# Attention and two MoE layers in one kernel: zero products on TensorE at the start, later weight conversion, and the first MoE units among the last pair's work

## The chip, the cores and the metric

One core of a Trainium2 chip runs the whole kernel in one launch. The metric is the device time in microseconds. Names of engines: PE is TensorE, DVE is VectorE, ACT is ScalarE, POOL is GpSimd, SP is the engine whose queue issues most DMAs.

## The reference

```python
def _attn_ref(q, k, v):                 # q, k, v: (4, 8, 576, 64) float32
    # rotary embedding on q and k: [x1*cos - x2*sin, x1*sin + x2*cos]
    scores = scale * np.matmul(q_rot, k_rot.transpose(0, 1, 3, 2))
    scores = scores - np.max(scores, axis=-1, keepdims=True)
    attn = np.exp(scores)
    attn = attn / (np.sum(attn, axis=-1, keepdims=True) + 1e-09)
    return np.matmul(attn, v)

x = attn_out.transpose(0, 2, 1, 3).reshape(2304, 512)
h = np.maximum(x @ w_in, 0.0)           # w_in (512, 2048), w_out (2048, 512)
x = (h * h) @ w_out
h = x @ w_in2                           # the second layer, alpha (2048,)
g = np.maximum(h, 0.0) + alpha * np.minimum(h, 0.0)
out = g @ w_out2
```

The weights arrive as 64-bit floats and are turned into 32-bit pairs on the chip.

## The kernel before

**Attention** goes over 16 pairs (one batch, two heads; a head in each half of the 128 partitions). For a pair POOL applies the rotary embedding (`rope`), PE transposes q and k (`turn`, steps KQ, X), ACT writes their rounded high part and DVE the residue (KH, KL, XK, XL, XQ, QL). `scores` (S) makes a block of 128 queries for one head, three matmuls for each half of the keys; the fifth block (i = 4) holds both heads' last 64 queries and reads the tile `qt` beside `nat`. DVE takes its maximum (`top`, R), ACT the exponential with its row sums (`exps`, E). PE transposes the exponentials (`trans`, T; U and W for tails) into banks of PSUM, ACT or DVE copy them out (C, CU, CW), and PE multiplies them with v (`pv`, PV). `store` (ST) and `over_leave` (OR) send the product and the inverse sums to DRAM.

The order on PE, POOL, DVE and ACT is written out by hand. `PLAN` gives each step of a pair a time in a period of 14.053 parts and for some an engine; pair n's step stands at n + time / 14.053 on a common axis, `at` pushes it into a heap, and `run` issues all in order of time. A pair's steps reach over nearly three periods, so up to four pairs overlap. The steps before time 0 of pair 0 are issued by hand at the start: k's rope, its transposes, then q in two parts (columns r = 0, 1 first), with the first score block between them. PSUM has eight banks: four for scores, three for transposes (`bank`), one (`acc`) for the products.

**The MoE layers** go by units. A unit of the first layer is one chunk of 128 hidden columns for 384 tokens: 12 matmuls (`products`, L785 to L787), a rectifier and a square on ACT (`finish`). The first 32 units take two token blocks by turns, so that unit t needs chunk t // 2. `Weights` converts a chunk in stages: load, `convert` and `mask` on DVE, `grow` on ACT, `sign` on DVE, `join` on ACT and DVE; six DVE instructions and two on ACT. Each unit has a list of such stages to issue behind it. The tokens of the first two blocks are read back from DRAM, multiplied by the inverse sums, rounded and split on POOL (`load_x`, `join_x`, `high_x`, `low_x`), through two buffers.

`moe` is a generator: attention resumes it by the event `follow`, 17 times for the tokens' split from 13.8 on (every 0.12 periods), then 11 times. The conversion of chunks 0 to 3 is spread over steps -9 to -1 of it. Two units (`EARLY`) are issued by the last two resumptions, at 17.9, behind everything of attention; the rest follows when attention is done. The scores' banks become the units' four banks (`ps_h`) after the last score; the other four (`ps_y`) are for the second product.

Of the kernel before, what the change touches and what calls it, by code (L numbers as in the profile page):

```python
# [56 lines left out]
AHEAD_X = 17  # L57
X_AT, X_EVERY = 13.8, .12
FOLLOW_AT = 15.5, 15.65, 15.9, 16.05, 16.2, 16.35, 16.5, 16.65, 16.8, 17.9, 17.91
ET = mybir.EngineType  # L60
FIRST_DONE = "KQ", "KH", "KL", "X0", "X1", "XK", "XL", "XQ", "QL", "S0", "R0", "E0"
MANUAL = {ET.PE, ET.Pool, ET.DVE, ET.Activation}


def attention(tc, q, k, v, ident_d, rope_d, xd, rd, follow):
# [10 lines left out]
    with ExitStack() as at:  # L76
        pool = lambda name, bufs, **kw: at.enter_context(tc.tile_pool(name=name, bufs=bufs, **kw))
        front = at.enter_context(ExitStack())
        fpool = lambda name, bufs, **kw: front.enter_context(tc.tile_pool(name=name, bufs=bufs, side="right", **kw))
        pp = pool("aP", NP_)  # L80
        pt = pool("apt", PTB)
        sm = pool("asm", 2)
        st_ = pool("asums", 1)
        ident = st_.tile([P, P], F32, name="ident")
        lds = [fpool("ald0", 1)]
# [24 lines left out]


        raw = {(x, nm): (st_ if nm == "v" else lds[0]).tile([P, 4, 5, D], F32, name=f"{nm}raw{x}") for x in range(2) for nm in "kqv"}
        for x in range(2):
# [18 lines left out]

        def first_rope(nm, r0, r1):

            w, E = r1 - r0, V
            x = raw[0, nm][:, 0:2, r0:r1]
            c, ns, s = (tab[:, r0:r1, i].unsqueeze(1).to_broadcast([P, 2, w, HALF]) for i in range(3))
            if (0, nm) not in rot:
                rot[0, nm] = rp.tile([P, 5, 2, D], F32, name=f"rot{nm}")
            r = rot[0, nm][:, r0:r1].rearrange("p r j d -> p j r d")  # L140
            t1, t2 = (rt.tile([P, 2, 5, D], F32, name=f"f{i}", bufs=1)[:, :, 0:w] for i in (1, 2))
# [181 lines left out]
        def over_leave(n):  # L323
            b, hp = pairs[n]
            r = sm.tile([9, P], F32, name="ri")
            A.activation(out=r, in_=turned.pop((n, "o"))[0:9, 0:P], func=AF.Copy)
            for j in range(2):
                nc.sync.dma_start(out=rd[hp, j, b * S:b * S + 512].rearrange("(i p) -> i p", i=4), in_=r[4 * j:4 * j + 4, :])
            nc.sync.dma_start(out=rd[hp:hp + 1, :, b * S + 512:b * S + 576], in_=r[8:9, :].rearrange("o (j c) -> o j c", j=2))

# [10 lines left out]
        def store(n, hf, side):  # L341
            b, hp = pairs[n]
            ready = n in sts
            if not ready:
                sts[n] = sm.tile([P, S], F32, name="st", bufs=1)
            high(sts[n][:, hf * SH:(hf + 1) * SH], acc.pop((n, hf))[:, 0:SH], side)
            if ready:
                nc.sync.dma_start(out=xd[:, hp, b * S:(b + 1) * S], in_=sts.pop(n))

# [10 lines left out]
        def run():  # L360
            while events:
                t, _, f, a = heapq.heappop(events)
                f(*a)

        def whole(gen):
# [23 lines left out]
        load(0, "q", 2, 4)  # L389
        first_rope("k", 0, 5)  # L390
        first_rope("q", 0, 2)
        for h in range(2):
            whole(turn(0, h, "k"))
            turn_high(0, h, "A", "k")
        whole(turn_tail(0, 0))
        ktail_high(0, "A")
        for h in range(2):
            turn_low(0, h, "k")
        ktail_low(0)
        for c0, c1 in ((0, 2), (2, 4)):  # L400
            if c0:
                first_rope("q", 2, 5)
                for kind, j in itertools.product("RE", range(2)):
                    queue(0, f"{kind}0{j}")
                run()
            for h in range(2):
                whole(turn(0, h, "q", c0, c1))
                turn_high(0, h, "A", "q", c0, c1)
            for h in range(2):
                turn_low(0, h, "q", c0, c1)  # L410
            if c0 == 0:
                for j in range(2):
                    queue(0, f"S0{j}")
                run()
                tables()
        whole(turn_tail(0, 1))
# [8 lines left out]
        for n in range(2, pairs_n):  # L425
            for w, name in ("k", "X0"), ("q", "X1"):
                at(n - 2 + PLAN[name][0] / PERIOD + .25 * (w == "k") + .01, rope, n, w)
            if n % 2 == 0 and n > 2:
                at(n - 3 + PLAN["X1"][0] / PERIOD + .02, load, n // 2, "k")
                at(n - 3 + PLAN["X1"][0] / PERIOD + .02, load, n // 2, "q")  # L430
                at(n - 3 + max(PLAN[x][0] for x in ("PV04", "PV14")) / PERIOD + .01, load, n // 2, "v")

        for n in range(pairs_n):
            for name in PLAN:
                if n or name[:2] not in FIRST_DONE:
                    queue(n, name)
        at(pairs_n - 3 + PLAN["X1"][0] / PERIOD + .02, front.close)
        at(pairs_n - 1 + max(PLAN[x][0] for x in PLAN if x[0] in "REKXQ" or x in ("S40", "S30", "S31")) / PERIOD + .001, scored.close)
        for x in range(AHEAD_X):
            at(X_AT + X_EVERY * x, follow)  # L440
        for x in FOLLOW_AT:
            at(x, follow)
        run()


NB, W = 6, 384
FIRST = 2
STEPS_AHEAD, EARLY = 8, 2
# [71 lines left out]
def moe(tc, xd, rd, mats, pbias, dram, al, out):  # L520
# [11 lines left out]
    with ExitStack() as mo:  # L532
# [240 lines left out]
        def products(u):  # L773
# [84 lines left out]
        conv = [[(d, lambda *j, f=f: f(st, *j)) for d, f in stages] for stages in weights.stages]  # L858
        before = {}
        for k in range(2 * FC):  # L860
            if k < HELD0:
                for d, (_, stage) in zip(FIRST_AT[k], conv[0][1:]):
                    if d < -STEPS_AHEAD - 1:
                        before.setdefault(AHEAD_X + STEPS_AHEAD + 1 + d, []).append((stage, (0, 0, k)))
                    else:
                        jobs.setdefault(d, []).append((0, stage, (0, 0, k)))
                continue
            at = EARLY + EVERY0 * (k - HELD0)
            if k >= FC + OUT0 + OUTX:
# [26 lines left out]
        for e in range(AHEAD_X):  # L896
# [4 lines left out]
            if e in (4, 6):  # L901
                weights.load(st, 0, 0, e // 6)
            for stage, j in before.get(e, []):
                stage(*j)
            yield
# [8 lines left out]
        for t in range(-STEPS_AHEAD - 1, NU + 1):  # L914
# [14 lines left out]
            unfinished += [t - 1] if 0 <= t - 1 < NU and not (t < NU and units[t][0] and units[t][2:] == (0, 0)) else []  # L929
            if "g0" in late:  # L930
                while unfinished:
                    finish(unfinished.pop(0))
# [3 lines left out]
            if t == at_unit[0, NB - 1, 1, 0]:  # L936
                open_two()
            for d, stage, j in sorted(jobs.get(t, []), key=lambda x: x[0]):
                stage(*j)
            if 0 <= t < NU:  # L940
# [8 lines left out]
def fused_kernel(ctx: ExitStack, tc: tile.TileContext, q, k, v, w_in1, w_out1, w_in2, w_out2, alpha, ident_d, rope_d, out):  # L949
# [9 lines left out]
    rest = moe(tc, xd, rd, ((w_in1, w_out1), (w_in2, w_out2)), pbias, dram, al, out)  # L959
    early = iter(range(AHEAD_X + STEPS_AHEAD + 1 + EARLY))  # L960

    def follow():
        if next(early, None) is not None:
            next(rest)

# [37 lines left out]
```

## Time and profile before

| | us |
|---|---|
| median of 3 runs (1070.88 to 1072.12) | 1071.8 |
| the profiled execution | 1077.4 |
| its span, first to last instruction | 1075.6 |
| PE busy in the span | 1035.5 (96%) |
| DVE busy | 717.6 (67%) |
| ACT busy | 584.6 (54%) |
| POOL busy | 379.8 (35%) |
| first unit of the MoE layers starts | 288.35 |

The profiled execution is 5.6 us longer than the median of the others. Times in the rows count from the first instruction. A PE record may be part of a product in 32-bit floats: one `pv` call on one half of the array leaves two records. PE and its weight load (PEld) overlap, and consecutive matmuls overlap by their ends.

### The profile page before, as it was taken

The page shows a single profiled execution, that of the slowest core. Times are in us where ns is not written, and L with a number is a line of the kernel's source. Part 1 is how long each engine was busy: PE and PEld are TensorE (multiplying, and loading weights), DVE is VectorE, ACT ScalarE, POOL GpSimd, SP SyncE. Part 2 cuts the span into 40 slices and gives each one's busy share as a digit, 9 for nine tenths or more (in the row PEclk, how much of TensorE's full clock was granted, in tenths as well). Part 3 has the DMA queues.
Part 4 walks back from the last instruction along what each step waited for, and adds up shares of the span by engine and source line. Part 5 has one row for each costly group of instructions (what it writes and reads, how often), then busy time and mean ns, then how long its engine had stood idle before and what let it go on. Part 6 is the DMA issues. An engine that isn't in the chain of part 4 may idle for free.

```text
span 1075.6 us, 19735 instructions
## 1 busy us (share of the span) xinstructions
PE 1035.5 (96%) x7296; PEld 927.4 (86%) x7296; DVE 717.6 (67%) x1270; ACT 584.6 (54%) x1283; POOL 379.8 (35%) x363
## 2 busy tenths in 40 slices
PE   4899999998999999999999999999999999999997
PEld 3677777775699999999999999899889998899886
DVE  5688888888489977797988876545444463644521
ACT  3688888886378644644646554444343442434321
POOL 6866667636000001332404223355311560136200
PEclk9899999998799999999999999899999999999999
DMA  7022232135434424556565566898214860268111
GB/s 187 2 79 68 90 90 77 60 104 168 127 117 139 134 89 135 186 184 215 192 213 198 185 205 217 316 301 268 63 59 139 254 216 1 59 210 253 37 30 30
DMA packets 101136, 153.21 MB, mean 142 GB/s; under 512 B 16944, under 2 KB 61360, under 8 KB 101040
## 3 DMA queue, kind: packets, MB, share of 16 engines
q1 hardware_dynamic: 100480, 151.41, 44.8%
q8 instruction: 58, 0.95, 0.4%
q10 hardware_dynamic: 560, 0.54, 0.2%
q14 instruction: 38, 0.31, 0.1%
HBM read 114.61 MB, written 37.30 MB: 141 GB/s over the span
## 4 chain that ended last, share of the span: by engine, by line
PE 62%; DVE 5%; DMA 3%; issue 2%; POOL 1%; ACT 1%; SPq 1%; POOLq 0%; DVEq 0%; ACTq 0%
PE py L804 23%; PE ph L697 16%; PE ph L804 8%; PE ph L787 5%; PE ph L785 5%; PE ph L786 5%; DVE gl L738 1%; DMA w<-in_moe_w_in_dram 1%; DVE m L494 1%; DMA xt<-x 1%; DVE m L493 1%; DMA w<-x 1%; DVE w L508 0%; DVE w L596 0%; DMA w<-in_moe_w_out_dram 0%
## 5 line engine op out<-in xcount | busy, mean ns | idle before, releaser
L738 DVE TENSOR_TENSOR gl<-g,gh 128x384 fp32r<-128x384 f32 x189 | 127.6, 680 | 118.0 <-PE py L804 97.0
L697 PE MATMUL ph<-T,xs 128*128 128x384 f32 x1008 | 175.9, 335 | 0.0
L697 PEld LDWEIGHTS ph<-T,xs 128*128 128x128 f32 x1008 | 175.1, 188 | 0.5 <-ACT w L689 0.2
L731 ACT ACTIVATE gh<-g 128x384 fp32r<-128x384 f32 x189 | 97.9, 521 | 142.0 <-PE py L804 137.8
L804 PE MATMUL py<-gh,w 128*128 128x384 f32 x560 | 145.7, 334 | 0.0
L260 DVE TENSOR_REDUCE nm<-sc 128x1 f32<-128x576 f32 x144 | 107.4, 755 | 38.7 <-PE sc L255 36.6
L785 PE MATMUL ph<-xs,held 128*128 128x384 f32 x384 | 128.3, 334 | 0.0
L786 PE MATMUL ph<-xs,held 128*128 128x384 f32 x384 | 128.3, 334 | 0.0
L787 PE MATMUL ph<-xs,held 128*128 128x384 f32 x384 | 128.3, 334 | 0.0
L255 PE MATMUL sc<-nat 64*128 64x288 f32 x768 | 120.0, 322 | 4.8 <-ACT p L269 4.3
L269 ACT ACTIVATE p<-sc,nm 128x576 f32<-128x576 f32 x144 | 105.6, 735 | 25.1 <-DVE nm L260 25.0
L255 PEld LDWEIGHTS sc<-nat 64*128 64x128 f32 x768 | 105.1, 201 | 7.1 <-ACT p L269 6.4
L804 PE MATMUL py<-w,gh 128*128 128x512 f32 x336 | 103.6, 389 | 0.0
L804 PEld LDWEIGHTS py<-gh,w 128*128 128x128 f32 x560 | 101.5, 188 | 0.0
L755 POOL TENSOR_TENSOR xt<-xt 128x384 f32<-128x384 f32 x24 | 27.9, 1166 | 197.0 <-DMA xt<-x 160.1
L804 PE MATMUL py<-gl,w 128*128 128x384 f32 x280 | 94.1, 336 | 3.2 <-DVE gl L738 3.1
L277 PE MATMUL ps<-ident,p 64*128 64x64 f32 x1152 | 92.8, 236 | 1.1 <-DVE ptt L177 1.1
L685 POOL TENSOR_TENSOR g<-g,m 128x384 f32<-128x384 f32 x62 | 67.8, 1101 | 74.0 <-ACT g L684 73.9
L277 PEld LDWEIGHTS ps<-ident,p 64*128 64x128 f32 x1152 | 83.6, 148 | 8.8 <-issue 7.4
L338 PE MATMUL acc<-pt,vraw 128*64 128x288 f32 x512 | 83.8, 441 | 0.9 <-ACT pt L175 0.6
L503 ACT ACTIVATE w<-w,pbias 128x512 uint32<-128x512 uint32 x64 | 48.7, 761 | 48.0 <-DVE w L499 43.7
L804 PEld LDWEIGHTS py<-w,gh 128*128 128x128 f32 x336 | 63.0, 188 | 13.1
(148 smaller groups left out, 2118.4 us busy)
## 6 DMA issues: line engine op xcount, KB each, us to landing
xs<-ws SPq DMA_DIRECT2D x168, 256.0 KB
w<-in_moe_w_in_dram SPq DMA_DIRECT2D x32, 512.0 KB
w<-in_moe_w_out_dram SPq DMA_DIRECT2D x32, 512.0 KB
ws<-w SPq DMA_DIRECT2D x40, 256.0 KB
wk<-xs SPq DMA_DIRECT2D x16, 512.0 KB
w<-wk SPq DMA_DIRECT2D x14, 512.0 KB
x<-st SPq DMA_DIRECT2D x16, 288.0 KB
xt<-x SPq DMA_DIRECT2D x24, 192.0 KB
```

Of the source, the lines that this page charges most:

```text
L255: T.matmul(t[:, x, 0:SH], lhsT=lhs, rhs=k[b][h, c0:c0 + SH], start=y == 0, stop=y == 2)
L260: V.tensor_reduce(out=nm[n, i, j], in_=sc[n, i, j][:, :, 0:SH], axis=AX.XY, op=ALU.max, negate=True)
L269: A.activation(out=Pt[n, i][:, j * S:(j + 1) * S].rearrange("p (a b) -> p a b", a=2), in_=sc.pop((n, i, j))[:, :, 0:SH], func=AF.Exp, bias ...
L277: T.transpose(u[:, 64 * k:64 * k + 64], Pt[n, i][halves[h], c0:c0 + P], ident[halves[h], halves[h]])
L338: T.matmul(acc[n, hf][64 * j:64 * j + 64, 0:SH], lhsT=v2[:, j, c], rhs=t, start=c == 0, stop=c == 4)
L697: T.matmul(bank[c], lhsT=w[:, y0, ws_], rhs=t[:, y1], start=first_ and kc == 0 and n == 0, stop=kc == 1 and n == 2, skip_group_check=not f ...
L731: A.activation(out=hi, in_=hidden(layer, b, i), func=AF.Copy)
L738: V.tensor_tensor(out=lo, in0=hidden(layer, b, i), in1=gsp[u][0].bitcast(F32), op=ALU.subtract)
L785: T.matmul(ph[:, :W], lhsT=wh[:, cs], rhs=xh, start=(c == 0), stop=False)
L786: T.matmul(ph[:, :W], lhsT=wh[:, cs], rhs=xl, start=False, stop=False)
L787: T.matmul(ph[:, :W], lhsT=wl[:, cs], rhs=xh, start=False, stop=(c == KC - 1))
L804: T.matmul(acc, lhsT=x, rhs=y, start=(s0 and k == 0), stop=(s1 and k == 2))
```

## The change

- The q rope is done in one piece behind the k rope, and POOL copies one element of its result (`last`) ahead of its own ropes. The tables are built ahead of both.
- PE runs products and transposes of a tile of zeros: 7 products (`spin`, two matmuls each) at the start and 2 behind k's transposes (`WARM`); then, for three pairs that don't exist (-3 to -1), a product in the place of each PV and eight transposes in the place of each T, from time 0 to the place of pair 0's first PV.
- The tokens' split starts at 13.5 instead of 13.8. The 25 further resumptions have written places in the last pair's period, in its plan's parts. Chunk 0 is converted from 12.91 on (the last maximum stands at 12.465), one stage per resumption.
- Four units are issued within attention, at 17.51, 20.9, 26.44 and 39.87. The four after them write the banks of `ps_y`.
- The stores of the last two pairs are issued by ACT's queue instead of SP's. The pool of exponentials (`aP`) is placed behind two others.

```diff
-X_AT, X_EVERY = 13.8, .12
-FOLLOW_AT = 15.5, 15.65, 15.9, 16.05, 16.2, 16.35, 16.5, 16.65, 16.8, 17.9, 17.91
+X_AT, X_EVERY = 13.5, .12
+FOLLOW_AT = (0, 12.38, 12.91, 14.33, 14.34, 15.59, 15.63, 17.51, 17.52, 17.68, 17.69, 19.61, 20.89, 20.9, 21.23, 24.16, 24.17, 25.21, 26.43, 26.44, 28.94, 29.68, 29.69, 31.73, 33.66, 39.87)
-FIRST_DONE = "KQ", "KH", "KL", "X0", "X1", "XK", "XL", "XQ", "QL", "S0", "R0", "E0"
+FIRST_DONE = "KQ", "KH", "KL", "X0", "X1", "XK", "XL", "XQ", "QL"
+WARM = 7, 2
...
+        zeros, last = st_.tile([P, SH], F32, name="zeros"), st_.tile([P, 1], F32, name="last")
+        idle = ps_a.tile([P, 512], F32, name="acc")
+        G.memset(zeros, 0.0)
...
+            eng = nc.scalar if n + 2 >= pairs_n else nc.sync      # over_leave; likewise in store
...
+        def spin():
+            for j in range(2):
+                T.matmul(idle[64 * j:64 * j + 64, 0:SH], lhsT=zeros[:, 0:64], rhs=zeros, start=True, stop=True)
+
+        def idle_turns(h):
+            u = bank()
+            for k in range(8):
+                T.transpose(u[:, 64 * k:64 * k + 64], zeros[halves[h], 0:P], ident[halves[h], halves[h]])
+                yield
...
-        first_rope("k", 0, 5)
-        first_rope("q", 0, 2)
+        tables()
+        for _ in range(WARM[0]):
+            spin()
+        first_rope("k")
         for h in range(2):
             whole(turn(0, h, "k"))
             turn_high(0, h, "A", "k")
         whole(turn_tail(0, 0))
         ktail_high(0, "A")
+        for _ in range(WARM[1]):
+            spin()
+        first_rope("q")
+        G.tensor_copy(out=last, in_=rot[0, "q"][:, 4, 1, 0:1])
         for h in range(2):
             turn_low(0, h, "k")
         ktail_low(0)
-        for c0, c1 in ((0, 2), (2, 4)):
...
+        for h in range(2):
+            whole(turn(0, h, "q"))
+            turn_high(0, h, "A", "q")
+        for h in range(2):
+            turn_low(0, h, "q")
...
+        for n in range(-3, 0):
+            for name in PLAN:
+                t = n + PLAN[name][0] / PERIOD
+                if t < 0 or t > min(PLAN[x][0] for x in PLAN if x[:2] == "PV") / PERIOD:
+                    continue
+                if name[:2] == "PV":
+                    at(t, spin)
+                elif name[0] == "T":
+                    steps(t, .063, idle_turns(int(name[2])), 8)
...
-        for x in FOLLOW_AT:
-            at(x, follow)
+        for x in FOLLOW_AT[1:]:
+            at(pairs_n - 1 + x / PERIOD, follow)
...
-STEPS_AHEAD, EARLY = 8, 2
+STEPS_AHEAD, EARLY = 0, 4
-FIRST_AT = (-9, -9, -9, -8, -8), (-7, -7, -7, -6, -6), (-5, -5, -5, -4, -4), (-3, -3, -3, -2, -2)
+FIRST_AT = -1, 0, 1, 2
...
-                ph = ps_h.tile([P, 512], F32, name="ph")
+                borrowed = EARLY <= u < EARLY + 4
+                ph = late["ps_y"].tile([P, 512], F32, name=f"py{u - EARLY}") if borrowed else ps_h.tile([P, 512], F32, name="ph")
...
-            at = EARLY + EVERY0 * (k - HELD0)
+            at = EARLY - 2 + EVERY0 * (k - HELD0)
...
+            for stage, j in first_jobs.get(t, []):
+                yield
+                stage(*j)
```

## Rows read from the trace of the kernel before

**Rows 1.** Waits of PE from 288 us on: total us, times, longest.
```profile
PE py L804 <- DVE gl L738: 4.5, 4, 1.8
```

**Rows 2.** Timeline, PE: start us, us, tiles; fifth score blocks of pairs 0, 1, 2, 14, 15.
```profile
29.51 1.81 PE L255 MATMUL sc<-nat,qt 128*128 128x288 f32 x6 [1.41 <-ACT p L269]
...
46.13 1.81 PE L255 MATMUL sc<-nat,qt 128*128 128x288 f32 x6 [1.41 <-ACT p L269]
...
63.19 1.05 PE L255 MATMUL sc<-nat,qt 128*128 128x288 f32 x6
...
240.97 1.05 PE L255 MATMUL sc<-nat,qt 128*128 128x288 f32 x6
...
259.20 1.32 PE L255 MATMUL sc<-nat,qt 128*128 128x288 f32 x6 [4.14 <-ACT p L269]
```

**Rows 3.** Windows, PE alone: stretch, its length, busy (instructions), granted clock, DMA.
```profile
44.00:46.00 2.00, 0.71 (x16) 0.69 0.04 8
...
50.00:52.00 2.00, 2.00 (x34) 0.60 0.00 0
```

**Rows 4.** Timeline, the start of pair 0.
```profile
5.86 1.70 DVE L144 TENSOR_TENSOR f<-kraw,tab 128x320 f32<-128x320 f32 x4 [5.86 <-DMA kraw<-in_k_dram]
...
7.59 0.82 DVE L145 TENSOR_TENSOR rotk<-f,f 128x640 f32<-128x640 f32 x1
...
9.72 0.94 DVE L183 TENSOR_TENSOR nat<-ps,nat 128x256 fp32r<-128x256 f32 x3
...
11.36 2.46 PE L255 MATMUL sc<-nat 64*128 64x288 f32 x12 [0.37 <-ACT nat L175]
11.55 3.17 DVE L144 TENSOR_TENSOR f<-qraw,tab 128x192 f32<-128x192 f32 x4
...
11.88 1.70 POOL L157 TENSOR_TENSOR t<-kraw,tab 128x640 f32<-128x640 f32 x1 [7.98 <-DMA kraw<-in_k_dram]
```

**Rows 5.** Timeline, PE: products with v at half and at full clock.
```profile
275.14 4.11 PE L338 MATMUL acc<-pt,vraw 128*64 128x288 f32 x16
...
285.77 2.16 PE L338 MATMUL acc<-pt,vraw 128*64 128x288 f32 x16 [0.56 <-ACT pt L175]
```

**Rows 6.** Timeline, POOL and DVE, tokens' split and first conversion.
```profile
233.93 1.01 POOL L755 TENSOR_TENSOR xt<-xt 128x384 f32<-128x384 f32 x1 [11.06 <-DMA xt<-r]
...
252.98 1.13 DVE L493 TENSOR_SCALAR m<-w 128x512 uint32<-128x512 uint32 x1
```

**Rows 7.** Windows: length, busy of PE, PEld, DVE, ACT, POOL, granted clock, DMA.
```profile
256.00:258.00 2.00, 0.00 (x0) 0.00 (x0) 1.85 (x4) 1.00 (x2) 1.94 (x2) 1.00 0.37 124
...
264.00:266.00 2.00, 2.00 (x24) 2.00 (x24) 0.79 (x2) 1.65 (x3) 0.00 (x0) 0.50 0.71 198
...
280.00:282.00 2.00, 1.71 (x16) 0.90 (x14) 0.22 (x1) 0.56 (x2) 0.00 (x0) 0.93 0.21 70
```

**Rows 8.** Groups by line, PE, from 259 to 288.35: busy us, mean ns, idle.
```profile
L338 PE MATMUL acc<-pt,vraw 128*64 128x288 f32 x64 | 13.5, 560 | 0.9 <-ACT pt L175 0.6 <-ACT st L175 0.3
L277 PE MATMUL ps<-ident,p 64*128 64x64 f32 x88 | 9.1, 300 | 1.1 <-DVE ptt L177 1.1
```

**Rows 9.** Timeline, a change of kind and eight transposes at full clock.
```profile
281.40 0.14 PEld L307 LDWEIGHTS ps<-ident,p 64*128 64x128 f32 x1 [0.44 <-issue]
...
281.52 0.66 PE L277 MATMUL ps<-ident,p 64*128 64x64 f32 x8
```

**Rows 10.** The chain that ended last, one of the units' matmuls: start us, us.
```profile
299.91 0.17 PE ph L787
```

**Rows 11.** Timeline, DVE: first and last of a chunk's six instructions.
```profile
274.31 0.42 DVE L493 TENSOR_SCALAR m<-w 128x512 uint32<-128x512 uint32 x1
...
277.93 0.69 DVE L515 SCALAR_TENSOR_TENSOR held<-m,w 128x512 fp32r<-128x512 f32 x1
```

**Rows 12.** Timeline, issues of two small stores; the first rectifier.
```profile
281.65 0.76 SPq L328 DMA_DIRECT2D r<-ri  x2
...
291.74 0.49 ACT L828 ACTIVATE g<-ph 128x384 f32<-128x384 f32 x1 [2.67 <-DMA r<-ri]
```

More of the change, by code (lines that the diff above doesn't have):

```diff
@@ L79, in attention @@
         fpool = lambda name, bufs, **kw: front.enter_context(tc.tile_pool(name=name, bufs=bufs, side="right", **kw))
-        pp = pool("aP", NP_)
         pt = pool("apt", PTB)
@@ L83, in attention @@
         st_ = pool("asums", 1)
+        pp = pool("aP", NP_)
         ident = st_.tile([P, P], F32, name="ident")
@@ L131, in load, with first_rope @@
             eng.dma_start(out=t[halves[nm == "q"], :, 4], in_=src[:, 512:576, :].rearrange("h p d -> p h d"))
[L133 to L141, printed above, removed]
+        def first_rope(nm):
+            E, w = V, 5
+            x = raw[0, nm][:, 0:2]
+            c, ns, s = (tab[:, 0:5, i].unsqueeze(1).to_broadcast([P, 2, w, HALF]) for i in range(3))
+            rot[0, nm] = rp.tile([P, 5, 2, D], F32, name=f"rot{nm}")
+            r = rot[0, nm].rearrange("p r j d -> p j r d")
+            t1, t2 = (rt.tile([P, 2, 5, D], F32, name=f"f{i}", bufs=1) for i in (1, 2))
             lo, hi = slice(0, HALF), slice(HALF, D)
@@ L326, in over_leave @@
             A.activation(out=r, in_=turned.pop((n, "o"))[0:9, 0:P], func=AF.Copy)
+            eng = nc.scalar if n + 2 >= pairs_n else nc.sync
             for j in range(2):
-                nc.sync.dma_start(out=rd[hp, j, b * S:b * S + 512].rearrange("(i p) -> i p", i=4), in_=r[4 * j:4 * j + 4, :])
-            nc.sync.dma_start(out=rd[hp:hp + 1, :, b * S + 512:b * S + 576], in_=r[8:9, :].rearrange("o (j c) -> o j c", j=2))
+                eng.dma_start(out=rd[hp, j, b * S:b * S + 512].rearrange("(i p) -> i p", i=4), in_=r[4 * j:4 * j + 4, :])
+            eng.dma_start(out=rd[hp:hp + 1, :, b * S + 512:b * S + 576], in_=r[8:9, :].rearrange("o (j c) -> o j c", j=2))
         def pv(n, hf, c):
@@ L347, in store @@
             if ready:
-                nc.sync.dma_start(out=xd[:, hp, b * S:(b + 1) * S], in_=sts.pop(n))
+                (nc.scalar if n + 2 >= pairs_n else nc.sync).dma_start(out=xd[:, hp, b * S:(b + 1) * S], in_=sts.pop(n))
         pairs_n = len(pairs)
@@ L399, in attention @@
         ktail_low(0)
-        for c0, c1 in ((0, 2), (2, 4)):
[L401 to L415, printed above, removed]
+        for h in range(2):
[3 more added lines that the diff above has]
+            turn_low(0, h, "q")
         whole(turn_tail(0, 1))
@@ L858, in moe @@
         conv = [[(d, lambda *j, f=f: f(st, *j)) for d, f in stages] for stages in weights.stages]
-        before = {}
+        first_jobs = {}
         for k in range(2 * FC):
             if k < HELD0:
[L862 to L866, printed above, removed]
+                first_jobs.setdefault(FIRST_AT[k], []).extend((stage, (0, 0, k)) for _, stage in conv[0][1:])
                 continue
-            at = EARLY + EVERY0 * (k - HELD0)
+            at = EARLY - 2 + EVERY0 * (k - HELD0)
             if k >= FC + OUT0 + OUTX:
@@ L902, in moe @@
                 weights.load(st, 0, 0, e // 6)
-            for stage, j in before.get(e, []):
-                stage(*j)
             yield
@@ L929, in moe @@
             unfinished += [t - 1] if 0 <= t - 1 < NU and not (t < NU and units[t][0] and units[t][2:] == (0, 0)) else []
+            if t == EARLY:
+                for d, stage, j in sorted(jobs.pop(t, []), key=lambda x: x[0]):
+                    stage(*j)
             if "g0" in late:
@@ L938, in moe @@
             for d, stage, j in sorted(jobs.get(t, []), key=lambda x: x[0]):
+                stage(*j)
+            for stage, j in first_jobs.get(t, []):
+                yield
                 stage(*j)
@@ L959, in fused_kernel @@
     rest = moe(tc, xd, rd, ((w_in1, w_out1), (w_in2, w_out2)), pbias, dram, al, out)
-    early = iter(range(AHEAD_X + STEPS_AHEAD + 1 + EARLY))
     def follow():
-        if next(early, None) is not None:
-            next(rest)
+        next(rest)
     attention(tc, q, k, v, ident_d, rope_d, xd, rd, follow)
```

## The prediction

> **What bounds the kernel now.** I read the waits first. From 288 us to the end TensorE (PE) waits for DVE 4.5 us in four places and otherwise runs through [rows 1]: the two MoE layers are a train of matmuls, and what moves their start moves the end by as much. So only the time before 288 us is open, and there I read the timeline for one row that recurs once per pair, the fifth score block (out sc, in nat,qt) [rows 2]. From pair 2 to pair 14 it comes every (240.97 - 63.19) / 12 = 14.82 us. Three stretches miss that pace. Pair 0 needs until 29.51; pairs 1 and 2 come after 16.62 and 17.06 us; pair 15 after 18.23.
>
> Next the clock. [...] Before pair 15's fifth block PE waits 4.14 us for one exponential [rows 2], whose maximum stands on DVE behind the conversion of the first weight chunk (1.13 us for an instruction that takes 0.42 when GpSimd is quiet) [rows 6, 11]. PE is empty for a whole window; after it the clock is 0.50 for some 20 us, although PE is busy for 2.00 of 2.00 us, and it rises at about 280.3 [rows 7].
>
> **The change, part by part.** Sums are against the profiled execution: span 1075.6, its own time 1077.4; the median of the other runs is 1071.8, and I subtract the saving from that.
>
> *The start.* The k rope stays: four multiplies in 1.70 us and an add of 0.82, from 5.86 to 8.41 [rows 4], gated by DMA. The q rope is now whole and takes the same 2.52 us, to about 10.95. In the kernel before its second part took 3.17 us for four multiplies of 192 columns, against 1.70 for four of 320, because GpSimd's own rope ran beside it [rows 4]; the one-element copy called last now holds GpSimd's rope until q is done, which is before 11.88, where it started anyway [rows 4], so pair 1's rope is not later. The tables move to an idle ScalarE before 9 us: free, since DVE's rope is what the next step waits for. Behind the q rope DVE has three k residues (0.94 us in all), the first of which frees the bank for q's transposes at 11.3; transposes, copies and residues of k took from 8.41 to 10.66, 2.25 us, and the first score needs only the transposes and copies of q, some 1.3. First scores therefore at about 12.6 instead of 11.36 [rows 4]: 1.2 lost. What is gained is that nothing is left behind them: block 1 no longer waits for a second half of q.
>
> The zeros' memset lies in the 5.86 us in which DVE waits for DMA [rows 4]: free. Seven zero products are 28 records; at half clock a record is 4.11 / 16 = 0.257 us, at full clock 2.16 / 16 = 0.135 [rows 5], 3.8 to 7.2 us in all; begun by 1.5 they end by 8.7 at the latest, and the first real transpose is ready at 8.4. Cost between 0 and 0.3 us; I take 0. Two more (0.5 to 1.0 us) lie while DVE ropes q: free.
>
> *Until the third pair.* 19 zero products and 80 zero transposes stand in the places that the missing earlier pairs' would have. PE then carries what it carries in the steady state, and the pace of that is 14.82 us a pair, which is less than 16.62 and 17.06, because those were at half clock with PE waiting for ScalarE. From the first score to the fifth block the plan has 12.24 of 14.05 parts of a period, 12.9 us. So the fifth blocks come at 25.5, 40.3 and 55.1 instead of 29.51, 46.13 and 63.19: 8.1 us earlier from pair 2 on. Bounds: 9 if unpaired slots (there are no zeros for sums and tails) let PE run ahead; the other end is below nothing, if PE stays at half clock with more to do (rival 3). I take 8.1, the steady state's own pace.
>
> *The last pair's scores.* The activations' split begins 0.3 periods earlier. GpSimd stood idle 11.06 us before its first multiply for it [rows 6], so it starts earlier by about that and is done about when the fifth block of pair 15 comes; the first conversion is put behind the last maximum. The 4.14 us wait goes and pair 15 takes 14.82 instead of 18.23: 3.4 saved. At most 4.1 [rows 2]; at the least 0 if the eight splits, each of which waits for the one two before on SP's queue, still beat with DVE.
>
> *The tail.* Before: 29.15 us from pair 15's fifth block (259.20) to the first unit (288.35), then four units. A unit is 12 matmuls of 0.17 us [rows 10], 2.1 us with what 0.17 leaves off; four are 8.3. So 37.5 us until the fifth unit. After: the four stand among the tail's products. PE's own work at full clock is 80 records of products at 0.135 = 10.8, about 100 transposes at 0.66 / 8 = 0.08 = 8.0 (88 in the main row) [rows 5, 8, 9], the fifth block 1.1: 19.9 if nothing overlaps, some 17 as the ends of groups overlap; with units 25 to 28. Changing between kinds costs 0.44 us of idle at full clock [rows 9], about ten times: 4.4, partly the cover of the copies. I take 30.5, saving 7.0. The low end of the saving is 0, the tail at half clock as now; the high end 12, PE without a gap. DVE would hold it at about 21 us: four conversions of six instructions, 0.42 to 0.69 us each, 3.4 per chunk without GpSimd beside it [rows 11], 13.4; half of a fifth chunk 1.5; two maxima and the copies some 6. So DVE is no bound, but units 0 and 2 stand in PE's queue ahead of real products and wait for chunks 0 and 1: the chain of one chunk was 4.3 us (274.31 to 278.62) [rows 11], and unit 0 stands 4.6 plan parts (4.9 us) behind its first instruction: a margin of 0.6 us.
>
> Stores of the last two pairs go from SP to ScalarE's queue: past the weight load that now waits on SP for a buffer. An issue is 0.38 us for a small one [rows 12], four per pair, 1.7 us of a ScalarE that is half idle there. At the end they stand ahead of the first rectifiers, and four units' worth of those (0.49 us each and a square) come at once, some 5.5 us with the issues. The next four units go to other banks and cover 8.3 us. Before, the first rectifier itself waited 2.67 us for such a store [rows 12]. The ninth unit needs chunk 4, whose join on ScalarE stands behind the burst: I charge 0.5.
>
> [...]
>
> Sum: 8.1 + 3.4 + 7.0 - 0.5 = 18.0 us. 1077.4 becomes 1059.4, the median 1053.8.
>
> **Rivals.** (1) *The clock falls between warm-up and scores.* From 8.4 to 12.6 PE has two groups of transposes and the two zero products, about half of the time, little more than in the window of the fall at 44.8 [rows 3]. Then the first 5.5 us of scores run at half speed, as from 46.13 to 51.6, 2.7 us lost: 1056.5. For it speaks that fall; against it, the stretch is shorter. (2) *Conversions gate the units.* PE stands at unit 0 or 2, the clock falls as it did behind the empty window, and the tail saves 1 to 3 instead of 7: 1059. For it: DVE was busy 1.85 of 2 us in that window [rows 7]; against: GpSimd no longer slows it. (3) *Slower: zeros that are paid at half clock.* If they fail to raise the clock, PE has two pairs' scores, 108 matmuls at 0.24 = 26 us (between 2.46 / 12 = 0.205 [rows 4] and 1.81 / 6 = 0.30 [rows 2], which has their end in it), and 19 x 4 x 0.257 = 19.5 us of zeros before pair 1's fifth block: 58 instead of 46.13, 12 later, and with ten changes of kind at double price 16. The rest gives 9.9 back: 6 us slower, 1078. It decides from about 20 us on, by whether the score matmuls there still take 0.24 us. Against it: at 51.6 the clock did rise under a mix of scores, transposes and products; for it: transposes and products alone kept PE busy from 264 to 280 at 0.50 [rows 7].
>
> [...]
>
> (4) *GpSimd is late.* Pair 1's two ropes take about 10 us from 11.0 (1.70 for the first of four instructions [rows 4], the two halves about one more, the add one more); their transposes come at about 22.5. If that rope or its bank is late by 3 us, every pair behind is: 1057. (5) *It doesn't do what it says*: the steady pace was set by something that zeros don't change and only the end gains: 1062.
>
> **How the numbers follow.** Forecast 0.50 (own range 1050.5 to 1056); rival 1 0.16; rival 2 0.13; rival 3 0.07; rival 4 0.06; rival 5 0.04; anything else 0.04, on either side. About 0.2%, 2.1 us, is what a measurement here can tell from no change. Faster: all but rival 3 and half of the rest, less a few for sums of two rivals: 0.89; same 0.04; slower 0.07. The range 1049.0 to 1063.0 takes rivals 1, 2, 4 and 5 in and leaves rival 3 and the tails out.
>
> **What would show it.** Fifth score blocks at about 25.5, 40.3, 55.1 and then every 14.8, each of 1.05 us from pair 0 or 1 on; no wait for an exponential near the last one; granted clock 1.00 from 52 to the first units; matmuls of units 0 to 2 among the last pair's products, the fifth unit at about 277 to 279. Wrong if the six matmuls of pair 1's block still take 1.8 us, if half clock shows in the tail, or if the fifth unit comes after 287.

## The result and the profile after

The changed kernel takes 1057.88 us (median of four runs, 1055.03 to 1063.79) against 1071.82 (1070.88 to 1072.12): 13.9 us less, ratio 0.9879, 95% interval 0.9836 to 0.9921. The forecast was 1053.8 us; its own range ended at 1056, the range at 1063. Direction and places are as forecast, the size is 4 us too large. The profiled execution took 1057.82 us, its span is 1056.0.

The timeline of TensorE (start us, duration, tiles, idle before and its releaser) shows the fifth score blocks of pairs 0, 1, 2, 14 and 15, the answer to [rows 2]:

```profile
27.87 1.06 PE L257 MATMUL sc<-nat,qt 128*128 128x288 f32 x6 [0.29 <-ACT p L271]
...
43.16 1.06 PE L257 MATMUL sc<-nat,qt 128*128 128x288 f32 x6 [0.30 <-ACT p L271]
...
57.99 1.06 PE L257 MATMUL sc<-nat,qt 128*128 128x288 f32 x6
...
235.83 1.06 PE L257 MATMUL sc<-nat,qt 128*128 128x288 f32 x6
...
250.22 1.06 PE L257 MATMUL sc<-nat,qt 128*128 128x288 f32 x6 [0.28 <-ACT p L271]
```

Every block now takes 1.06 us, and the 4.14 us wait before the last is 0.28. Pair 2 is 63.19 - 57.99 = 5.2 us earlier than before, pairs 2 to 14 keep 14.82 us a pair, and pair 15 takes 14.39 instead of 18.23, another 3.8.

In the tail the four units (out ph, line 803) stand among pair 15's products; here are the first matmuls of the first, second and fourth, and of the fifth unit (out py):

```profile
259.49 0.44 PE L803 MATMUL ph<-xs,held 128*128 128x384 f32 x1
...
265.47 0.45 PE L803 MATMUL ph<-xs,held 128*128 128x384 f32 x1
...
281.10 0.42 PE L803 MATMUL ph<-xs,held 128*128 128x384 f32 x1
...
283.27 0.33 PE L803 MATMUL py<-xs,held 128*128 128x384 f32 x1
```

From the last fifth block to the fifth unit it is 33.05 us. Before, the fifth unit's first matmul stood at 296.80:

```profile
296.80 0.33 PE L785 MATMUL ph<-xs,held 128*128 128x384 f32 x1
```

That is 37.6 us behind the last fifth block, so 4.5 saved. Together 5.2 + 3.8 + 4.5 = 13.5; some 0.4 remains for all that follows.

Windows of after (stretch, length, busy us and instructions of PE, PEld, DVE, ACT, POOL, granted clock, DMA share, GB/s): two at the start, one inside its slow stretch and one at its end, one at the first conversion, and the tail as a whole.

```profile
10.00:12.00 2.00, 0.66 (x8) 0.35 (x5) 1.97 (x6) 0.00 (x0) 0.64 (x2) 0.92 0.99 290
12.00:14.00 2.00, 1.63 (x13) 1.45 (x13) 1.05 (x5) 1.04 (x4) 2.00 (x3) 0.50 1.09 268
...
16.00:18.00 2.00, 2.00 (x10) 0.65 (x9) 0.41 (x1) 1.40 (x4) 1.92 (x3) 0.50 0.46 27
18.00:20.00 2.00, 2.00 (x33) 1.93 (x35) 0.77 (x2) 0.00 (x0) 1.92 (x3) 0.87 0.67 189
...
254.00:256.00 2.00, 0.99 (x14) 0.78 (x13) 2.00 (x4) 0.43 (x1) 0.60 (x2) 1.00 0.46 133
...
250.22:283.27 33.05, 28.76 (x237) 20.45 (x238) 22.33 (x43) 13.59 (x29) 4.67 (x5) 1.00 0.50 157
```

The clock falls to 0.50 at about 11.7 us, ahead of the first score, and is full again from about 18.5: rival 1. In the tail, which ran at 0.50 for some 20 us before [rows 7], it is 1.00 throughout. There PE is busy 28.76 of 33.05 us, and its waits from 250 to 283.3 us (total, times, longest) are nearly all for copies of transposes (two of 0.3 us are left out):

```profile
PE ps L279 <- ACT pt L177: 1.6, 2, 1.1
PE acc L341 <- ACT pt L177: 1.3, 2, 1.1
PE ps L279 <- DVE ptt L179: 1.0, 1, 1.0
```

From 280 us to the end, one row, against [rows 1]:

```profile
PE py L822 <- DVE gl L755: 3.2, 3, 1.8
```

### The profile page after: what moved, and what is told of

Same layout as the page of the kernel before. It is cut to its first block, busy times and chain, and to the rows that moved or that the text cites. A ratio compares the mean times of both kernels' runs of the same rounds, so it can differ in the third digit from the quotient of the medians.

```text
span 1056.0 us, 20115 instructions
## 1 busy us (share of the span) xinstructions
PE 1035.4 (98%) x7488; PEld 922.4 (87%) x7488; DVE 710.3 (67%) x1263; ACT 585.4 (55%) x1281; POOL 376.3 (36%) x365
## 4 chain that ended last, share of the span: by engine, by line
PE 88%; DVE 4%; DMA 3%; ACT 2%; issue 1%; POOL 1%; SPq 1%; ACTq 0%; POOLq 0%; DVEq 0%
PE py L822 26%; PE ph L714 17%; PE ph L822 9%; PE acc L341 6%; PE sc L257 6%; PE ph L803 6%; PE ph L805 6%; PE ph L804 6%; PE ps L279 3%; DMA xt<-r 1%; PE ps L198 1%; DVE nm L262 1%; PE acc L370 1%; DVE gl L755 1%; DMA w<-x 1%
## 5 line engine op out<-in xcount | busy, mean ns | idle before, releaser
L755 DVE TENSOR_TENSOR gl<-g,gh 128x384 fp32r<-128x384 f32 x189 | 129.8, 691 | 118.8 <-PE py L822 102.6
L803 PE MATMUL ph<-xs,held 128*128 128x384 f32 x368 | 123.3, 335 | 0.0
L805 PE MATMUL ph<-xs,held 128*128 128x384 f32 x368 | 122.9, 334 | 0.0
L804 PE MATMUL ph<-xs,held 128*128 128x384 f32 x368 | 122.9, 334 | 0.0
L257 PE MATMUL sc<-nat 64*128 64x288 f32 x768 | 114.3, 310 | 0.5 <-ACT nat L177 0.4
L257 PEld LDWEIGHTS sc<-nat 64*128 64x128 f32 x768 | 99.9, 190 | 2.2 <-ACT p L271 1.5
L279 PE MATMUL ps<-ident,p 64*128 64x64 f32 x1152 | 86.8, 226 | 2.6 <-ACT pt L177 1.6
L279 PEld LDWEIGHTS ps<-ident,p 64*128 64x128 f32 x1152 | 77.8, 139 | 10.6 <-issue 7.3
L341 PE MATMUL acc<-pt,vraw 128*64 128x288 f32 x512 | 79.5, 422 | 1.7 <-ACT pt L177 1.3
L803 PEld LDWEIGHTS ph<-xs,held 128*128 128x128 f32 x368 | 69.1, 188 | 0.6 <-issue 0.4
```

What stands on the lines that cost most here:

```text
L257: T.matmul(t[:, x, 0:SH], lhsT=lhs, rhs=k[b][h, c0:c0 + SH], start=y == 0, stop=y == 2)
L279: T.transpose(u[:, 64 * k:64 * k + 64], Pt[n, i][halves[h], c0:c0 + P], ident[halves[h], halves[h]])
L341: T.matmul(acc[n, hf][64 * j:64 * j + 64, 0:SH], lhsT=v2[:, j, c], rhs=t, start=c == 0, stop=c == 4)
L755: V.tensor_tensor(out=lo, in0=hidden(layer, b, i), in1=gsp[u][0].bitcast(F32), op=ALU.subtract)
L803: T.matmul(ph[:, :W], lhsT=wh[:, cs], rhs=xh, start=(c == 0), stop=False)
L804: T.matmul(ph[:, :W], lhsT=wh[:, cs], rhs=xl, start=False, stop=False)
```

## The experiments

All were timed, four to six times each, beside the kernel before (medians 1071.3 to 1072.7 us in the three sets); a ratio is to the kernel before of the same set. "Bridge" is the fourth kernel, after with `WARM = 10, 5`; from the fifth on (but for the seventh) it is the base.

**1 and 2. Each half alone.** `e1_front_only` is the kernel before with the new start and the zeros; `e2_tail_only` is after with the old start and no zeros.

> The start of the change alone (whole q rope, GpSimd's rope held off, zero products and transposes), the tail as before. Theory (the start, the last pair and the tail each save by themselves): the fifth blocks of pairs 0, 1, 2 at 27.9, 43.2, 58.0 as in the changed kernel, pair 15's again about 18 behind pair 14's, half clock in the tail, and 5 us less than before: 1066 to 1067. Rival (the start's gain is eaten where the conversions meet the scores of the last pair): 1070 to 1072.

> The tail of the change alone (tokens' split and conversions moved, four units among the last pair's products, stores on ScalarE), the start as before and no zeros. Theory: fifth blocks at 29.5, 46.1, 63.2 as before, pair 15's 14.4 behind pair 14's, no half clock in the tail, 8 to 9 us less than before: 1063. Rival (the tail gains only because the start leaves the clock or DVE in another state): under 5 us, 1067 or more.

In short, not as the lines stand, against after:

```
e1:  -X_AT = 13.5 ; STEPS_AHEAD, EARLY = 0, 4 ; FIRST_AT = -1, 0, 1, 2 ; new FOLLOW_AT
     +X_AT = 13.8 ; STEPS_AHEAD, EARLY = 8, 2 ; the old tables and stores
e2:  -WARM, zeros, last, spin, idle_turns, the loop over n in range(-3, 0)
     +first_rope(nm, r0, r1) and the two halves of q, as before
```

Measured: e1 1064.77 us, ratio 0.9937 [0.9921, 0.9953]; e2 1064.95, 0.993 [0.9913, 0.9946]. Each saves about 6.5, together 13 of the 13.9: the halves nearly add. Both times miss their expected ranges, e1 by saving more than its theory's 5 us, e2 by saving less than its 8 to 9. In e1 pair 15's fifth block waits 3.62 us for its exponential and comes 17.75 us behind pair 14's; in e2 it comes after 14.74 with 0.27 of waiting. So the 3.8 us of pair 15 belong to the half with the earlier split and the later conversion, not to the start. The tail of e1, whose code is that of before, took 34.4 us in its profile, against 37.6 in before's (mean granted clock there 0.73): the 4.5 us that after saves there are measured against one profile, and these two of the same tail differ by 3.2.

**3. Without the fill.** Warm-up stays, the zeros in the missing pairs' places go.

> The changed kernel without the zeros of the three missing pairs; the nine warm-up products stay. Theory (the fill brings and holds the clock): scores at half clock again, the fifth block of pair 2 at 61 to 63 instead of 58.0, 3 to 5 us more than the changed kernel: 1061 to 1063. Rival (the start gains by the whole q rope and GpSimd held off, and zeros only cost PE time): no change or faster, fifth block of pair 2 at 56 to 58, 1056 to 1058.

```
-        for n in range(-3, 0):
-            ...
-                if name[:2] == "PV":
-                    at(t, spin)
-                elif name[0] == "T":
-                    steps(t, .063, idle_turns(int(name[2])), 8)
```

Measured: 1063.02 us, 0.9912 [0.9896, 0.9928]. Its fifth blocks:

```profile
28.17 1.81 PE L257 MATMUL sc<-nat,qt 128*128 128x288 f32 x6 [1.41 <-ACT p L271]
...
46.64 1.81 PE L257 MATMUL sc<-nat,qt 128*128 128x288 f32 x6 [1.41 <-ACT p L271]
...
63.49 1.05 PE L257 MATMUL sc<-nat,qt 128*128 128x288 f32 x6
```

Pair 2 is where the kernel before had it (63.19), half a us past the expected range. The whole gain of the start is the fill's; the whole q rope and the warm-up bring nothing without it.

**4. A longer warm-up.** Three more zero products before the first rope, three more before the second.

> The changed kernel with 10 and 5 warm-up products instead of 7 and 2, which closes most of the two gaps of PE before the first score. Theory (the granted clock falls at 11.8 because of them, and the spread of the changed kernel's times, 1055 to 1064, is whether and how long it does): clock 1.00 through 10 to 20 us, fifth block of pair 2 at about 55.2, times of 1053 to 1056 with a spread under 3 us. Rival (the fall comes anyway, or the added products delay the first score): fifth block of pair 2 at 58 or later, 1057 to 1060.

```
-WARM = 7, 2
+WARM = 10, 5
```

Measured: 1055.68 us (1055.04 to 1056.69), 0.9849 [0.9831, 0.9866]. The window of after's fall, then the ten first scores in after (13.15) and in the bridge (13.35), and the bridge's first and third fifth blocks:

```profile
10.00:12.00 2.00, 2.00 (x20) 1.01 (x15) 1.97 (x5) 0.44 (x2) 0.47 (x2) 1.00 0.89 273
```

```profile
13.15 1.98 PE L257 MATMUL sc<-nat 64*128 64x288 f32 x10 [0.37 <-ACT nat L177]
```

```profile
13.35 1.31 PE L257 MATMUL sc<-nat 64*128 64x288 f32 x10 [0.67 <-ACT nat L177]
...
26.22 1.06 PE L257 MATMUL sc<-nat,qt 128*128 128x288 f32 x6 [0.29 <-ACT p L271]
...
56.48 1.07 PE L257 MATMUL sc<-nat,qt 128*128 128x288 f32 x6
```

With PE busy 2.00 instead of 0.66 us in the window of the fall, the clock stays at 1.00; the same ten scores take 1.31 us instead of 1.98, so this does not rest on the record of the clock alone. Pairs 0 to 2 come 1.5 to 1.7 us earlier. Rival 1 priced this at 2.7, and the expectation had pair 2 at 55.2: it came 1.3 later. The intervals of after's and this ratio overlap, so it is the trace, not the time alone, that places the gain; the spread of its runs is 1.65 us against 8.8.

**5 and 6. Which zeros.** Both on the bridge: the 19 zero products alone, and the 80 zero transposes alone.

> The kernel with 10 and 5 warm-up products, but of the fill only the 19 zero products, no zero transposes. Theory (products and scores carry the clock, transposes add little): granted clock 1.00 from 14 to 50 us, fifth block of pair 2 at 56 to 57 as in the bridge, 1055 to 1057. Rival (the transposes are needed, as PE has gaps without them): the clock falls between 16 and 46, fifth block of pair 2 at 58.5 or later, 1058 or more.

> The same with only the 80 zero transposes in the fill, no zero products there. Theory (transposes do little for the clock, as in the tail of the kernel before): the clock falls between 14 and 45, fifth block of pair 2 at 60 to 63.5, 1060 to 1063. Rival (any instruction that keeps PE busy holds the clock): 1.00 throughout, 56 to 57, 1055 to 1057.

```
e5:  -                elif name[0] == "T":
     -                    steps(t, .063, idle_turns(int(name[2])), 8)
e6:  -                    at(t, spin)
     +                    continue
```

Measured: products alone 1056.2 us, 0.9851 [0.983, 0.9871]; transposes alone 1061.36, 0.9892 [0.9873, 0.9911]. Fifth blocks of pairs 0 to 2 with products alone:

```profile
25.62 1.05 PE L257 MATMUL sc<-nat,qt 128*128 128x288 f32 x6 [0.29 <-ACT p L271]
...
40.36 1.06 PE L257 MATMUL sc<-nat,qt 128*128 128x288 f32 x6 [0.29 <-ACT p L271]
...
55.19 1.05 PE L257 MATMUL sc<-nat,qt 128*128 128x288 f32 x6
```

These are the forecast's 25.5, 40.3 and 55.1, a us earlier than expected of this experiment. With the transposes in (the bridge) the first interval is 15.29 us, without them 14.74: the zero transposes cost 1.3 us by pair 2 and buy nothing. From pair 0 to pair 2 it is 30.1 to 30.6 us in the eight kernels whose clock is full there and that have them, 29.6 in the two without (this one and experiment 12). The whole time does not show it (1056.2 against 1055.68). With transposes alone, windows of the start:

```profile
14.00:16.00 2.00, 0.78 (x16) 0.64 (x12) 1.49 (x3) 0.82 (x3) 1.92 (x2) 0.92 1.24 239
...
20.00:22.00 2.00, 2.00 (x29) 2.00 (x27) 0.57 (x1) 0.66 (x2) 1.92 (x2) 0.50 0.49 150
```

PE idles for 1.3 us, which the products would have filled, the clock falls in that hole at about 15.7 us, and it is still 0.50 in a window in which PE is busy for all of 2.00 us with scores and transposes. It recovers, and falls once more at about 26, where PE is busy for 0.59 of 2 us. Pair 2's block comes at 61.27. That transposes as such do less for the clock than products, the theory of this experiment, is not shown by it: after's clock, too, reads 0.50 from 16 to 18 us with PE busy throughout, and there zero products fill the time: it fell at 11.7 and was full again from 18.5, here it fell at 15.7 and was full again from 22.5. The stretch of before's tail [rows 7] holds transposes and products mixed. What the two fills differ in here is that the transposes alone leave holes.

**7. Without warm-up.** After with `WARM = 0, 0`.

> The changed kernel with no warm-up product at all, the fill as changed. Theory (the clock fell before the first scores anyway, so 7 and 2 buy little): scores start at half clock, full clock from 18 to 20, fifth blocks as in the changed kernel's profile within 0.7 us (pair 2 at 57.5 to 58.7), 1057 to 1060. Rival (the warm-up is what lets the clock come back so soon): full clock only after 22, pair 2 at 60 or later, 1061 or more.

Measured: 1060.47 us, 0.9883 [0.9864, 0.9902]. The fifth blocks come at 27.80, 43.09 and 58.34, within 0.4 us of after: a warm-up whose clock falls again before the first score is worth nothing at the start. (The record reads 1.00 there, but its window from 16 to 18 us holds ten PE records, as after's does at 0.50.) The times show no difference either: this kernel saves 12.2 us on the kernel before of its set, after 13.9, and the intervals overlap. In its trace the clock falls in the tail:

```profile
254.00:256.00 2.00, 1.21 (x19) 1.07 (x19) 2.00 (x4) 0.39 (x2) 0.57 (x1) 1.00 0.54 141
256.00:258.00 2.00, 2.00 (x15) 0.88 (x14) 1.67 (x3) 1.72 (x4) 1.02 (x1) 0.68 0.29 105
258.00:260.00 2.00, 1.81 (x17) 1.60 (x16) 1.87 (x6) 1.08 (x4) 0.24 (x1) 0.50 0.09 34
```

and its tail lasts 34.75 us instead of 33.05, though its units stand where after's do. After has 0.99 us of work where this kernel has 1.21, and did not fall. Why this one fell is open, and the warm-up cannot be its cause by any path that the traces show.

**8. Units at the end.** The bridge with units 0 to 2 issued beside unit 3, behind all of pair 15's products.

> 10 and 5 warm-up products; the first three units are issued at 39.87 beside the fourth, behind the last pair's work, with the conversions left where they are. Theory (the units fill waits of the tail and keep the clock up): the last four stand in a row, the wait for copies stays, the clock falls in the tail, and the fifth unit comes 4 to 8 us later: 1060 to 1064. Rival A (units fill waits, but the clock stays up without them): 2 to 4 us later, 1057.5 to 1060. Rival B (each unit costs its own time and two changes of kind): no change, 1055 to 1057.

```
-                products(t)
+                for u in range(EARLY) if t == EARLY - 1 else [t] * (t >= EARLY):
+                    products(u)
```

Measured: 1059.64 us, 0.9882 [0.9864, 0.9901]. The tail takes 35.39 us instead of the bridge's 31.71, and the clock falls in it:

```profile
270.00:272.00 2.00, 0.28 (x5) 0.14 (x3) 1.37 (x4) 1.51 (x4) 0.00 (x0) 0.93 0.56 197
272.00:274.00 2.00, 1.54 (x8) 0.94 (x10) 1.93 (x4) 0.35 (x2) 0.00 (x0) 0.50 0.01 4
```

The theory held but for its size: the fifth unit comes 3.9 us later, not 4 to 8. In the tail PE waits 6.2 us for copies of transposes and products (2.2, 1.8, 1.5 and 0.7 us), in the bridge 3.1. So the units fill waits where they stand, and without them the clock fell (0.28 us of work in the window of the fall); that they always keep it is not shown, since it fell in experiment 7 with the units in place.

**9. Half of the split.** The bridge without the second token block's loads and split.

> 10 and 5 warm-up products; the load and split of the second token block are left out, its first-layer units read the first block's split (so half of that work on GpSimd and SP is gone). Theory (GpSimd's split is still running when the first chunk is converted, and that is part of what the tail took more than forecast): GpSimd is done before 245, no conversion instruction over 0.75 us, from pair 15's fifth block to the fifth unit 30 to 31.2 us instead of 31.7 to 33.1, 1054 to 1055. Rival (the tail's time is the chain of transposes, copies and products, and the changes of kind): 31.5 or more, 1055 to 1056.5.

```
-            for k in range(FIRST * KC):
+            for k in range(KC):
-                for c, (xh, xl) in enumerate(xsp[layer, b]):
+                for c, (xh, xl) in enumerate(xsp[layer, 0 if first(layer, b) else b]):
```

Measured: 1057.96 us, 0.9862 [0.9843, 0.9882]: no gain, and past both expected ranges. GpSimd's last instruction of the split starts at 240.76 instead of 253.23, and the tail is 31.6 us against 31.7: what is left of the tail's shortfall in the bridge is not GpSimd. Pair 15 became slower, 16.68 us. The timeline of SP, DVE and PE says why:

```profile
237.16 5.72 SPq L766 DMA_DIRECT2D xt<-r x6
242.98 0.54 SPq L351 DMA_DIRECT2D x<-st  x1
```

```profile
246.11 0.46 DVE L179 COPY st<-acc 128x288 f32<-128x288 f32 x1 [2.78 <-DMA x<-st]
...
246.72 1.68 PE L341 MATMUL acc<-pt,vraw 128*64 128x288 f32 x12 [1.90 <-DVE st L179]
```

Six small loads hold SP for 5.72 us, some 2.4 more than three times the 1.09 that two took at 232.74. GpSimd's instruction of 240.76, which reads what such loads bring, ends at 241.77, and 1.1 us later, the time of two loads, SP is through: so I take it that the last two waited for that instruction. Pair 13's store is issued behind them, its buffer st comes free late, DVE's copy into it waits 2.78 us and PE 1.90 for the bank. Thinning the queue put a load that had to wait in front of a store.

**10. Stores back on SP.**

> 10 and 5 warm-up products; the last two pairs' stores back on SP's queue. Theory (they stand behind a weight load that waits for a buffer, and the next copy waits for the store's buffer): stores of pair 14 several us late, PE waits for a product copy, 1 to 4 us more: 1057 to 1060. Rival (no one waits for them): 1055 to 1056.5, or up to 0.5 us less, since ScalarE has no issues ahead of the first rectifiers.

```
-            eng = nc.scalar if n + 2 >= pairs_n else nc.sync
+            eng = nc.sync
```

(and the same for the store of st). Measured: 1056.04 us, 0.9846 [0.9827, 0.9866], fifth unit at 280.91 as in the bridge (280.95). The move of the stores is worth nothing.

**11. Without the hold.** The bridge without the one-element copy called last.

> 10 and 5 warm-up products; without the one-element copy that holds GpSimd's rope until q's rope is done. Theory (DVE and GpSimd slow each other): q's rope takes 3 to 5 us instead of 2.5, first score 0.5 to 2.5 us later than 13.35, 1056.5 to 1058. Rival (GpSimd waits for its data until about 11 anyway): first score at 13.1 to 13.5, no change.

```
-        G.tensor_copy(out=last, in_=rot[0, "q"][:, 4, 1, 0:1])
```

Measured: 1064.1 us, 0.9919 [0.9903, 0.9936]: 8 us slower than the bridge. Its timeline, beside after's three instructions of the same kind:

```profile
7.76 1.67 POOL L159 TENSOR_TENSOR t<-kraw,tab 128x640 f32<-128x640 f32 x1 [3.58 <-DMA qraw<-in_q_dram]
8.07 2.04 DVE L147 TENSOR_TENSOR rotk<-f,f 128x640 f32<-128x640 f32 x1
...
10.20 5.54 DVE L146 TENSOR_TENSOR f<-qraw,tab 128x320 f32<-128x320 f32 x4
...
18.96 1.33 PE L257 MATMUL sc<-nat 64*128 64x288 f32 x5 [0.37 <-ACT nat L177]
```

```profile
7.79 0.82 DVE L147 TENSOR_TENSOR rotk<-f,f 128x640 f32<-128x640 f32 x1
...
8.71 1.70 DVE L146 TENSOR_TENSOR f<-qraw,tab 128x320 f32<-128x320 f32 x4
...
11.33 0.19 POOL L415 COPY last<-rotq 128x1 f32<-128x1 f32 x1 [7.16 <-DVE rotq L147]
```

Beside GpSimd's rope DVE's multiplies take 5.54 instead of 1.70 us and the add 2.04 instead of 0.82, and the first score comes at 18.96 instead of 13.35, 5.6 us later and not the 2.5 at most that the theory had. The other 2 us are the clock: in this kernel it is 0.50 from 18 to 24 us, in the bridge it never falls, and pair 0's fifth block comes at 33.90 against 26.22. The four multiplies take 3.8 us more together, while each of GpSimd's instructions beside them lasts 1.1 to 1.7 us; by what the two engines hold each other up is not shown.

**12. Products alone, and unit 3 earlier.** Experiment 5 with the fourth unit at 34.4 instead of 39.87 of the plan.

> A version that may beat both: 10 and 5 warm-up products, the fill without transposes, and the fourth unit at 34.4 (behind the last transposes, where PE waits 1.1 us for their copy) instead of 39.87. Theory: fifth block of pair 2 at 55.2, the last wait for a copy gone, the fifth unit 1 us sooner after pair 15's fifth block than 32.2: 1053.5 to 1055. Rival (the unit delays the last products and their stores): 1055.5 to 1057.

```
-..., 29.69, 31.73, 33.66, 39.87)
+..., 29.69, 31.73, 33.66, 34.4)
```

Measured: 1056.76 us, 0.9855 [0.9835, 0.9876], no better. Pair 2's block comes at 54.89 as expected, but the tail takes 32.30 us, as long as in experiment 5 (32.21). The fifth unit, at 279.56, now waits itself:

```profile
279.56 0.45 PE L801 MATMUL py<-xs,held 128*128 128x384 f32 x1 [0.99 <-ACT ri L328]
```

Unit 3, the fourth, had covered the release of the bank that the fifth borrows; moved forward, it left that wait bare. The bridge, experiment 5 and experiment 10 remain the fastest, within each other's spread; their medians lie some 2 us under the changed kernel's, with intervals that overlap its own.

## Why the prediction was right, and where it was 4 us too large

The time lies in the stated range because that range was drawn to take in rivals 1, 2, 4 and 5; my own range ended at 1056 and missed it.

*The start: forecast 8.1, measured 5.2.* The mechanism held: the kernel loses its half-speed pairs only with the zeros (experiment 3), and rival 3 is excluded by blocks of 1.06 us from pair 0 on. The step that failed is the one that took the clock for full behind the warm-up. Rival 1, at a chance of 0.16, is what the profiled run shows; by the bridge it cost 1.5 us at pair 2, against the 2.7 that I gave it. I had compared the stretch with the window of the fall at 44.8 [rows 3] (a mean of 0.69 from 44 to 46 us puts the fall from 1.00 to 0.50 there, and 0.60 from 50 to 52 the return at 51.6) and set it aside as shorter; it was less busy too (0.66 us against 0.71). The rest, 1.3 us, is the zero transposes, which I had counted as part of the steady pace; with products alone the blocks stand within 0.1 us of the forecast. The first score came at 13.15 to 13.35 and not at 12.6, and that did no harm. (Rival 3's price counts ten changes of kind once, not at the double price it names; 16 would be about 21. No chance hung on it.)

*The hold.* Its forecast cost, nothing, is right, its reason was not. I argued from before's 11.88 us that GpSimd would not start earlier anyhow. But that start was the tables' doing, though [rows 4] puts it down to a DMA. In before ScalarE built them behind the first copies, and GpSimd began at 11.88, as the first was done:

```profile
11.21 0.59 ACT L103 ACTIVATE tab<-tab 128x480 f32<-128x480 f32 x1
```

With the tables moved forward GpSimd is ready at 7.76 (experiment 11). The copy is worth 8 us, more than any other single line here: when one step moves, the start time of what stood behind it can no longer be read from the trace of before.

*Pair 15: forecast 3.4, measured 3.8*, with the wait gone as described, though the split did not end as early as I had it. Before, its last instruction started at 261.69, after at 255.67: 6 us earlier, while the fifth block moved up 9. So GpSimd still ran beside the first conversion, 5.4 us behind that block. DVE's first two conversion instructions and GpSimd's in after:

```profile
252.40 1.01 DVE L510 TENSOR_SCALAR m<-w 128x512 uint32<-128x512 uint32 x1
...
253.09 1.18 POOL L772 TENSOR_TENSOR xt<-xt 128x384 f32<-128x384 f32 x1
253.44 1.37 DVE L511 SCALAR_TENSOR_TENSOR m<-w,m 128x512 f32<-128x512 uint32 x1
```

*The tail: forecast 30.5 us, measured 33.05.* In the bridge the same two conversions take 0.46 and 0.69 us, PE's 1.0 us wait for ptt is gone, and the tail is 31.71: about 1.3 of the 2.5 us missing is that contention. Experiment 9 bears it out: there the first chunk's six DVE instructions take 0.42 to 0.69 us, in the bridge 0.42 to 0.71, and its tail lasts 31.64; in after three of them take 1.4 us more in all. The other kernels with the units in place lie between, at 31.65 (experiments 3 and 10) and 32.2 to 32.4 (2, 5, 6, 11 and 12); only 7, whose clock fell, is beyond after. The remaining 1.2 us is in PE's own work (busy 28.6 us in the bridge, where I had 25 to 28) and in its waits for ScalarE's copies (2.9 us in after, 2.8 in the bridge), which I had covered in part by the changes of kind; experiment 9 rules GpSimd out for it. Rival 2 (a unit waits for its chunk) did not happen: none of the four units' rows has a wait. That the changes of kind around the four units make it up is not shown. The fourth unit is followed by the fifth, so there are seven changes to and from units; one shows 0.44 us of idle ahead of its weight load, three show 0.25, and experiment 8, with six of the seven gone, was slower.

*The burst on ScalarE: charged 0.5, measured none.* From 280 us on PE waits only for DVE's gl, three times instead of four; the fourth, and a wait of 1.3 us for ScalarE's gh that [rows 1] leaves out, lie in the stretch of the next paragraph. The stores' move, part of the same step, is free because it does nothing (experiment 10).

*The base.* The terms of the trace add up to 13.5 us at the fifth unit, close to the 13.9 of the medians; but the two profiled spans differ by 19.6. The other 6 lie behind the change, nearly all in before's profile alone. Its window there, and that of after:

```profile
660.00:680.00 20.00, 17.39 (x91) 16.82 (x90) 10.27 (x15) 7.59 (x18) 6.88 (x7) 0.91 0.94 337
```

```profile
660.00:680.00 20.00, 20.00 (x116) 19.82 (x116) 14.05 (x22) 7.98 (x18) 5.25 (x5) 1.00 0.95 342
```

A gap of 2.6 us and a clock of 0.91 stand there. The other runs of that kernel, 5.6 us shorter, have no profile here; but from the fifth unit to the end of the span it is 772.7 to 774.5 us in all thirteen other profiles and 778.8 in before's, so some 5 of the 5.6 belong to this one execution. Taking the saving off the median was right.

*Open.* Whether transposes keep the clock as products do; why the clock fell in the tail of experiment 7 and not of after; what the 1063.79 us run of after lost, which has no profile (its mean granted clock was 0.990 against 0.995); how the tail's last 1.2 us divide between PE's work, the copies and the changes of kind.

## What to carry to other kernels

Filling an engine's gaps with idle work paid here, where a gap went with the loss of a clock level, but only as far as the filler reached without a hole to the first real work and left none in it: the clock fell to 0.50 in a window with 0.66 us of work in 2 (after) and in a hole of 1.3 us (experiment 6), and stayed at 1.00 with 2.00 of 2 (experiment 4). The zero products did all of it, and the zero transposes, which alone left holes, only took time, 1.3 us by pair 2. When a step is moved, ask anew when everything behind it can start: the earliest start in the old trace may have been the moved step's doing, and a one-element copy that holds an engine back can be the dearest line of the change, here 8 us. Put short independent matmuls between products that wait for copies rather than behind them: here they filled waits, and where they were moved away PE waited 6.2 us for copies instead of 3.1 and the clock fell to 0.50 (experiment 8).

## What the runs showed of the hardware

Before its first change the record of the granted clock read 1.00 where matmuls ran at the slower pace: in the kernel before, six score matmuls took 1.81 us in pair 0 at a recorded 1.00, the same 1.81 in pair 1, where it reads 0.50, and 1.05 in pair 2 at 1.00 [rows 2]. Under matmuls on zeros alone the pace rose. In after nothing but zero products runs on PE until 8.67 us; the first twelve records of them take 3.15 us, all 28 take 5.43, and eight later ones 1.19, all at a recorded 1.00:

```profile
1.16 3.15 PE L370 MATMUL acc<-zeros 128*64 128x288 f32 x12 [1.16 <-POOL zeros L115]
...
9.12 1.19 PE L370 MATMUL acc<-zeros 128*64 128x288 f32 x8
```

GpSimd's rope beside DVE's stretched DVE's four multiplies 3.3 times (5.54 against 1.70 us, experiment 11 against after) and its own instructions by less (1.67 against 1.54, 1.43 against 0.86). And in experiment 9 loads that took 5.72 us instead of some 3.3 held the store behind them on their queue, and made DVE wait 2.78 us for the store's buffer and TensorE 1.90 for DVE.
